# Seven block products on three PSUM banks: another order of products, evictions, masks and stores in an attention and FFN kernel

## The chip, the core and the metric

The kernel runs on one core of a Trainium2 chip. A core has TensorE (PE, with its weight loads listed as PEld), VectorE (DVE), ScalarE (ACT), GpSimd (POOL) and SyncE (SP), which here only issues transfers. Time is the device time of one execution in microseconds; lower is better. Beside it stands the span: from the first to the last instruction that the hardware profiler recorded in one execution.

## What is computed

Attention with two kinds of masks, then a feed-forward layer, on 8 batches of 576 tokens, 8 heads of 64:

```python
scores = scale * np.matmul(q, k.transpose(0, 1, 3, 2))
rel = pos[:, None] - pos[None, :]
mask_plain = (rel >= 0) & (rel < 32)                        # heads 0 to 3
mask_dil = (rel >= 0) & (rel < 128) & (rel % 4 == 0)        # heads 4 to 7
attn = softmax(np.where(masks, scores, -1e9))
x = matmul(attn, v) as (4608 tokens, 512)
h = np.maximum(x @ w_in, 0.0)                               # w_in 512 x 2048
out = h * h @ w_out                                         # w_out 2048 x 512
```

The output is 4608 x 512 in float32; the matmuls run in bfloat16.

## The kernel before

The 4608 tokens go through the feed-forward layer in nine tiles of 512. For a tile the first matmul (`mm1`, L963) makes 16 blocks of 128 hidden features, four matmuls each. ACT takes each block from PSUM with a Relu (L993) and DVE squares it (L996) into `h2T`. The second matmul then sums over the 16 blocks. Attention for a batch runs between: the list `steps` (L1317 to L1394) tells behind which group of matmuls which step of attention is issued, and `natural_step` (L697) issues it. A step is a visit of PE (`V`, function `quadrants`, matmuls at L377) with scores for some head pairs and products with V for others; or the exponential and mask of a pair (`E`, ACT at L740, DVE at L742); or a logarithm of the sums (`L`, L708 and L709); or a reciprocal by an exponential and the multiplication into `xT`, the feed-forward layer's input (`X`, ACT L723, DVE L726 and L730). The order within an engine is the order of issue: nothing is reordered later. Waits are set where a tile is read, written or its buffer reused, and PE, ACT and DVE each go through their queues in order.

Batch 7, the last, has its two visits inside the seventh tile: one between the two matmuls of the feed-forward layer, one in the middle of the second. They are the last attention work; tiles eight and nine are feed-forward alone.

In the last three tiles (`fast`, L954) the second matmul is done in blocks of two by two with seven products in place of eight. Hidden features (low, high) and the tokens' two interleaved halves make four blocks a11, a12, a21, a22 of `h2T`; `w_out` has four blocks b11 to b22. `add_up` (L1022) makes on DVE the sums s1 = a21 + a22, a21 := a11 - a21, s2 = s1 - a11 and s4 = a12 - s2, in three pieces, behind blocks 7, 11 and 15. `weigh` makes the four sums of weights ahead of time. The products, 16 matmuls of 256 columns each, are M1 = a11 b11, M2 = a12 b21, M3 = s4 b22, M4 = a22 w4, M5 = s1 w1, M6 = s2 w2, M7 = a21 w3, and the four quarters of the output are

```
c11 = M1 + M2                  c12 = M1 + M6 + M5 + M3
c21 = M1 + M6 + M4 + M7        c22 = M1 + M6 + M7 + M5
```

`PRODUCTS` (L1085) gives the order, M1, M2, M6, M4, M7, M5, M3, and the PSUM bank of each. Banks come from the pool `ps_f` with four buffers, which also serves `mm1` and the visits. M6 is added by PE onto M1's bank, so that this bank holds M1 + M6; each of the others has its own. `after` (L1048) takes products out: ACT copies M1 and later M1 + M6 into `snap`, DVE adds banks and `snap` into `whole`, a float32 image of the tile's output, whose four row blocks hold every fourth token. `keep` stores one row block of `whole` per transfer, from SP (L944). In the last tile M3 comes in three pieces with a bank each, and the stores are cut by quarters.

The names by which the profile shows the sums: s1 and s2 lie in `qb`, s4 in `kb`; w1 and w2 lie in `qb`, w3 and w4 in `kb`.

Of the kernel before, what the change touches and what calls it, by code (L numbers as in the profile page):

```python
# [63 lines left out]
def kernel(  # L64
# [631 lines left out]

    def natural_step(b: int, code: str):  # L697
        what, e = code[0], int(code[1])
        if what in "QKR":
            arrange(b, what, e, int(code[2]), *(int(x) for x in code[3:4]), *[nc.scalar.copy][: len(code) - 4])  # L700
        elif what == "V":
            scs, pvs = ([(int(x[0]), int(x[1])) for x in y.split(",") if x] for y in code[2:].split("/"))
# [17 lines left out]
        elif what == "X":  # L720
            o, _, rest = op.pop((b, e))
            rec = recs.pop((b, e))
            nc.scalar.activation(rec[:, :], rec[:, :], ACT.Exp, scale=-1.0)  # L723
            t0 = b * M % (RING // RES)
            tok = xT[:, e, :, t0 : t0 + M]
            nc.vector.tensor_tensor(out=tok[:, :, 16:M], in0=byr(o[:, :]), in1=byr(rec[:, 0:512]), op=ALU.mult)  # L726
            for g, rows in enumerate(sides) if rest[0][0] is not rest[0][1] else [(0, slice(0, P))]:
                if rest[0][0] is not rest[1][0]:
                    g = g ^ crossed(b, e)
                nc.vector.tensor_tensor(  # L730
                    out=tok[rows, :, 0:16], in0=byr(rest[0][g][rows, :]), in1=byr(rec[rows, 512:576]), op=ALU.mult
                )
        else:
            g = int(code[2])
            second = g ^ ((b, e) == (NATURAL, 1))
            if not second:
                pts[b, e] = p_pool.tile([P, 896], bf16, name="pt")
            n = 384 if e >= NE // 2 else (448, 384)[g]
            pt = pts[b, e][:, 448 * g : 448 * g + n]
            nc.scalar.activation(pt, sp[b, e][g][:, 0:n], ACT.Exp, scale=SCALE)  # L740
            mask = (mask_f if e >= NE // 2 else mask_p[:, 384:] if b == XB else mask_n)[:, 0:n]
            nc.vector.tensor_tensor(out=pt, in0=pt, in1=mask, op=ALU.mult)  # L742
# [15 lines left out]

    far_blocks = [[(0, 0, 0, 64)], [(0, 16, 64, 112), (1, 80, 80, M)]]
    recs, turned = {}, set()  # L760
    first = {}
    held = []
    sides = [slice(64 * hl, 64 * hl + 64) for hl in range(2)]
# [176 lines left out]
    def store(osb, parts, *cuts):  # L940

        for x, n, row in parts:
            for c0, c1 in zip(cuts, cuts[1:]):
                nc.sync.dma_start(out[row : row + RES * (n - 1) + 1 : RES, c0:c1], osb[x : x + n, c0:c1])  # L944

    def ffn_groups(tk0: int, nt: int):
# [16 lines left out]
        def mm1(u, ks):  # L963
# [51 lines left out]
        sums_at = {7: (0, 4), 11: (4, 6), 15: (6, 8)}  # L1015

        def quarter(f0, f1, high, j):
# [4 lines left out]
        def add_up(f0, f1):  # L1022
# [3 lines left out]
            for to, one, two_, op in (  # L1026
                (s1, a21, a22, ALU.add),
                (a21, a11, a21, ALU.subtract),
                (s2, s1, a11, ALU.subtract),
                (s4, a12, s2, ALU.subtract),  # L1030
            ):
                nc.vector.tensor_tensor(out=to, in0=one, in1=two_, op=op)  # L1032

        final = tk0 + nt == NTOK
# [3 lines left out]
        def plus(to, one, two_):  # L1038
            nc.vector.tensor_tensor(out=to, in0=one, in1=two_, op=ALU.add)  # L1039

        def keep(rows, *cuts):
            for m in rows:
                parts = [(0, half, tk0 + m + RES * half), (half, half, tk0 + m)] if over else [(0, P, tk0 + m)]
                store(whole[:, m, :], parts, *cuts)

        halves = (0, HD, DM)

        def after(name, pieces=None):  # L1048

            bank = {k: t[:, :, :] for k, t in cur.items()}  # L1050
            if name == "M1":
                nc.scalar.copy(snap[0][:, :, :], bank["X"])  # L1052
            elif name == "M2":
                plus(c11, bank["Z"], snap[0][:, :, :])
                if final:
                    keep((0, 2), 0, HD)
            elif name == "M6":
                nc.scalar.copy(snap[1][:, :, :], bank["X"])
            elif name == "M4":
                plus(c21, bank["W"], snap[1][:, :, :])  # L1060
            elif name == "M7":
                plus(c21, bank["V"], c21)
                if final:
                    keep((1, 3), 0, HD)
            elif name == "M5":
                plus(snap[0][:, :, :], bank["Y"], snap[1][:, :, :])
                plus(c22, bank["V"], snap[0][:, :, :])
                keep((1, 3), *((HD, DM) if final else (0, DM)))
# [7 lines left out]
        def summed(x):  # L1076
            return lambda f, i: h_sum[x][:, f, P * i : P * i + P]
# [4 lines left out]
        def w_of(x):  # L1082
            return lambda f: w_sum[x][:, f, :]

        PRODUCTS = {  # L1085
            "M1": ("X", raw(0, 0), w_raw(0, 0)),
            "M2": ("Z", raw(1, 0), w_raw(1, 0)),
            "M6": ("X", summed(1), w_of(1)),
            "M4": ("W", raw(1, 1), w_of(3)),
            "M7": ("V", raw(0, 1), w_of(2)),  # L1090
            "M5": ("Y", summed(0), w_of(0)),
            "M3": ("Q", summed(2), w_raw(1, 1)),
        }
        ITEMS = [(name, f, i, 0, HD) for name in PRODUCTS for f in range(NF // 2) for i in range(2)]
        if final:
            ITEMS[-NF:] = [
                ("M3", f, i, y0, y1) for i, y0, y1 in ((0, 0, HD), (1, 0, HD // 2), (1, HD // 2, HD)) for f in range(NF // 2)
            ]

        def g2_fast(n):  # L1100

            head_ = 4 * NF
            lo, hi = (8 * n, 8 * n + 8) if n < 8 else (head_ + 6 * n - 48, head_ + 6 * n - 42 if n < 15 else len(ITEMS))
            for name, f, i, y0, y1 in ITEMS[lo:hi]:
                bank, lhs, rhs = PRODUCTS[name]
                piece = final and name == "M3"
                begin = f == 0 and (piece or i == 0) and name != "M6"
                if begin:
                    cur[bank] = ps_f.tile([P, 2, HD], f32, name="pf")
                nc.tensor.matmul(  # L1110
                    cur[bank][:, i, y0:y1], lhs(f, i), rhs(f)[:, y0:y1], start=begin, stop=f == NF // 2 - 1, skip_group_check=True
                )
# [220 lines left out]
    for b in range(NATURAL, B):  # L1333
# [35 lines left out]
            norm(1, t + 25)  # L1369
        else:  # L1370
            visit(t + 15, [(b, 3), (b, 1)], [(b, 0), (b, 2)][: 1 + (b >= PAIRED)])
            steps.extend((t + 15, 3, b, f"E1{x}") for x in range(2))
            if b >= PAIRED:
                norm(2, t + 15)
            expo(3, t + 16, t + 16)
            norm(0, t + 17)
            visit(t + 23, [(b + 1, 2), (b + 1, 0)] if after else [], [(b, 1), (b, 3)])
            if after:
                steps.extend((t + 23, 3, b + 1, f"E0{x}") for x in range(2))
                steps.extend((t + 27 + 2 * x, 1, b + 1, f"E2{x}") for x in range(2))  # L1380
            norm(3, t + 23)
            norm(1, t + 24)
# [62 lines left out]
```

## Time and profile before

| | |
|---|---|
| median of three runs | 293.96 us (293.78 to 298.44) |
| the profiled execution | 294.17 us, span 292.4 us |
| PE busy | 282.7 us, 97% |
| DVE busy, ACT busy | 183.5 us, 184.4 us, 63% each |
| seventh tile, second matmul with both visits | about 219.8 to 235.8 us |
| eighth tile | 235.8 to 261.8 us |
| ninth tile to the end | 261.8 to 292.4 us |

A row of a timeline gives start, busy time, engine, line and operation, `out<-in` with shapes, a count, and in brackets how long the engine had been idle and what ended that. A row of the waits gives the sum, the count and the longest. A modelled end stands behind each matmul: matmuls overlap, so their starts tell the pace. DMA rows give the size of a transfer and the median time from issue to landing.

### The profile page before, as it was taken

The page shows a single profiled execution, that of the slowest core. Times are in us where ns is not written, and L with a number is a line of the kernel's source. Part 1 is how long each engine was busy: PE and PEld are TensorE (multiplying, and loading weights), DVE is VectorE, ACT ScalarE, POOL GpSimd, SP SyncE. Part 2 cuts the span into 40 slices and gives each one's busy share as a digit, 9 for nine tenths or more (in the row PEclk, how much of TensorE's full clock was granted, in tenths as well). Part 3 has the DMA queues.
Part 4 walks back from the last instruction along what each step waited for, and adds up shares of the span by engine and source line. Part 5 has one row for each costly group of instructions (what it writes and reads, how often), then busy time and mean ns, then how long its engine had stood idle before and what let it go on. Part 6 is the DMA issues. An engine that isn't in the chain of part 4 may idle for free.

```text
span 292.4 us, 8216 instructions
## 1 busy us (share of the span) xinstructions
PE 282.7 (97%) x3361; PEld 179.7 (61%) x3377; DVE 183.5 (63%) x494; ACT 184.4 (63%) x375; POOL 123.2 (42%) x208
## 2 busy tenths in 40 slices
PE   8899999999999999999999999999998999999994
PEld 7589746959555544555455455555556865885683
DVE  2676315646769665686749577975388457643943
ACT  6788627777747864988667666667566547307510
POOL 8685266755553892876774679100000000000000
PEclk9999999999999999999999999999999999999999
DMA  8999999999999999999999499202100040003013
GB/s 123 196 172 205 205 218 203 187 159 164 168 210 153 180 125 206 115 171 201 125 219 166 50 138 221 23 2 102 43 1 2 4 143 0 2 28 115 2 36 108
DMA packets 84180, 35.77 MB, mean 122 GB/s; under 512 B 53296, under 2 KB 79536, under 8 KB 84144
## 3 DMA queue, kind: packets, MB, share of 16 engines
q0 software_dynamic: 49056, 18.49, 58.4%
q1 hardware_dynamic: 34944, 16.67, 28.8%
q8 instruction: 26, 0.43, 0.6%
q10 hardware_dynamic: 144, 0.10, 0.1%
q14 instruction: 10, 0.08, 0.1%
HBM read 37.50 MB, written 9.44 MB: 161 GB/s over the span
## 4 chain that ended last, share of the span: by engine, by line
PE 88%; DVE 5%; DMA 2%; ACT 2%; issue 1%; POOL 1%; DVEq 0%; POOLq 0%
PE pf L980 39%; PE pf L1148 28%; PE pf L1110 11%; DMA kb<-in_k_dram 2%; PE po L377 2%; DVE h2T L996 2%; PE pa L377 1%; PE pf L377 1%; DVE qb L1032 1%; ACT h2T L993 1%; PE pd L377 1%; PE pa L804 1%; ACT pt L740 1%; DVE kb L1032 1%; PE pf L856 0%
## 5 line engine op out<-in xcount | busy, mean ns | idle before, releaser
L980 PE MATMUL pf<-xT,w_in 128*128 128x512 bf16 (+1 forms) x704 | 128.0, 341 | 0.0
L993 ACT ACTIVATE h2T<-pf 128x512 bf16<-128x512 f32 x143 | 84.0, 602 | 42.3 <-PE pf L980 42.1
L980 PEld LDWEIGHTS <-w_in 128*128 128x128 bf16 x704 | 78.2, 114 | 45.7 <-issue 0.3
L1148 PE MATMUL pf<-w_out_sb,h2T 128*128 128x512 bf16 x368 | 84.1, 379 | 1.4 <-issue 0.6
L996 DVE TENSOR_TENSOR h2T<-h2T 128x512 bf16<-128x512 bf16 (+1 forms) x123 | 55.9, 468 | 33.4 <-ACT h2T L993 31.7
L1148 PEld LDWEIGHTS <-h2T 128*128 128x128 bf16 x384 | 36.5, 98 | 42.3
L329 POOL DMA_DIRECT2D vbd<-in_v_dram x80 | 43.2, 550 | 23.9 <-DMA qb<-in_q_dram 10.8
L1154 ACT COPY osb<-pf 128x512 f32<-128x512 f32 x22 | 12.9, 585 | 20.8 <-PE pf L1148 20.8
L1110 PEld LDWEIGHTS <-h2T 128*128 128x128 bf16 x192 | 18.6, 98 | 2.6
L723 ACT ACTIVATE rec<-rec 128x576 f32<-128x576 f32 x24 | 16.4, 685 | 0.7
L740 ACT ACTIVATE pt<-pa 128x384 bf16<-128x384 f32 (+1 forms) x26 | 11.8, 499 | 6.7 <-DVE xT L730 6.0
L183 POOL DMA_DIRECT2D kb<-in_k_dram x19 | 13.1, 691 | 6.7 <-DMA w_in<-in_moe_w_in_dram 3.2
L205 POOL DMA_DIRECT2D vbd<-in_v_dram x16 | 11.0, 694 | 11.7 <-DMA kb<-in_k_dram 7.8
L183 POOL DMA_DIRECT2D qb<-in_q_dram x19 | 13.5, 712 | 4.7 <-DMA xx<-qb 2.6
L321 POOL DMA_DIRECT2D vbd<-in_v_dram x20 | 12.0, 610 | 7.0 <-DMA qb<-in_q_dram 2.6
L726 DVE TENSOR_TENSOR xT<-po,rec 128x512 bf16<-128x512 f32 x13 | 9.0, 691 | 6.9 <-ACT rec L723 6.6
L1039 DVE TENSOR_TENSOR whole<-pf,snap 128x512 f32<-128x512 f32 (+2 forms) x14 | 8.2, 612 | 7.9 <-PE pf L1110 7.8
L1110 PE MATMUL pf<-qb,qb 128*128 128x256 bf16 x96 | 11.5, 272 | 1.5 <-ACT snap L1052 1.5
L315 POOL DMA_DIRECT2D vd<-in_v_dram x20 | 12.1, 614 | 1.4 <-issue 0.5
L742 DVE TENSOR_TENSOR pt<-pt,mask_f 128x384 bf16<-128x384 bf16 x24 | 8.4, 355 | 6.4 <-ACT pt L740 6.3
L726 DVE TENSOR_TENSOR xT<-pf,rec 128x512 bf16<-128x512 f32 x11 | 7.6, 691 | 7.6 <-ACT rec L723 7.6
L742 DVE TENSOR_TENSOR pt<-pt,mask_n 128x384 bf16<-128x384 bf16 (+1 forms) x20 | 7.1, 373 | 7.5 <-ACT pt L740 7.4
(176 smaller groups left out, 382.2 us busy)
## 6 DMA issues: line engine op xcount, KB each, us to landing
out_dram<-osb SPq DMA_DIRECT2D x24, 128.0 KB, 5.0
out_dram<-osb SPq DMA_DIRECT2D x12, 256.0 KB, 4.7
qb<-in_q_dram POOLq DMA_DIRECT2D x7, 320.0 KB, 11.3
kb<-in_k_dram POOLq DMA_DIRECT2D x7, 320.0 KB
vd<-in_v_dram POOLq DMA_DIRECT2D x34, 64.0 KB, 6.2
w_out_sb<-in_moe_w_out_dram POOLq DMA_DIRECT2D x4, 512.0 KB
out_dram<-whole SPq DMA_DIRECT2D x8, 256.0 KB, 3.0
qb<-in_q_dram POOLq DMA_DIRECT2D x6, 256.0 KB, 6.3
```

Source lines behind the costliest of these rows:

```text
L183: nc.gpsimd.dma_start(t[p0 : p0 + n, part, h0:h1, :], src[b, h0:h1, t0 : t0 + RES * n, :].rearrange("h (p r) d -> p h (r d)", r=RES),)
L329: nc.gpsimd.dma_start(v_rows[b % 2][p0 + 16 * r : p0 + 16 * r + 16, e, :, :], v[b, 2 * e + hl, :, :].rearrange("(i m r) d -> r m i d", r=R ...
L377: nc.tensor.matmul(out, lhs, rhs, start=begin, stop=True, skip_group_check=True)
L723: nc.scalar.activation(rec[:, :], rec[:, :], ACT.Exp, scale=-1.0)
L726: nc.vector.tensor_tensor(out=tok[:, :, 16:M], in0=byr(o[:, :]), in1=byr(rec[:, 0:512]), op=ALU.mult)
L740: nc.scalar.activation(pt, sp[b, e][g][:, 0:n], ACT.Exp, scale=SCALE)
L742: nc.vector.tensor_tensor(out=pt, in0=pt, in1=mask, op=ALU.mult)
L980: nc.tensor.matmul(to, w_in_sb[piece][:, kt, c0 : c0 + 509 : 4], rhs, start=(kt == kts[0] and x == 0), stop=(kt == kts[-1] and x == per - ...
L993: nc.scalar.activation(hv, acc[u][:, :].rearrange("p (x n) -> p x n", x=per), ACT.Relu)
L996: nc.vector.tensor_tensor(out=hv, in0=hv, in1=hv, op=ALU.mult)
L1110: nc.tensor.matmul(cur[bank][:, i, y0:y1], lhs(f, i), rhs(f)[:, y0:y1], start=begin, stop=f == NF // 2 - 1, skip_group_check=True)
L1148: nc.tensor.matmul(cur[m][:, c0:c1], h2[:, f, P * m : P * m + P], w_out_sb[:, f, c0:c1], start=(f == 0), stop=(f == NF - 1),)
```

## The change

- The order of the products becomes M1, M5, M6, M3, M7, M2, M4, on three banks: X takes M1, then M6, M7 and M4 on top of it, Y takes M5 and M3 on top, Z takes M2. X and Y are allocated together, Y first, ahead of M1. PE adds four products onto a bank in use where it added one, and DVE does three sums per tile where it did six.
- Evictions: ACT copies X behind M1 into c11, Y behind M5 into c22, X behind M6 into c12 and X behind M4 into c21. DVE adds Y to c12 behind M3, X to c22 behind M7, Z to c11 behind M2. `snap` goes.
- In the last tile M4 comes in the three pieces, now all on bank X, each copied by ACT.
- `keep` stores two row blocks (0 and 2, or 1 and 3) in one transfer.
- In the seventh tile: pair 1 of batch 7 does its second half's exponential first; its masks (`m`) are issued later than its exponentials (`e`); pair 3's exponentials and pair 0's normalisation come one and two groups later; the last `add_up` does s1 and s2 first and a21 and s4 (`Z0`) behind the masks.

```diff
-    snap = [const.tile([P, 2, HD], f32, name=f"snap{x}") for x in range(2)]
...
-            second = g ^ ((b, e) == (NATURAL, 1))
-            if not second:
-                pts[b, e] = p_pool.tile([P, 896], bf16, name="pt")
+            second = g ^ ((b, e) in ((NATURAL, 1), (B - 1, 1)))
             n = 384 if e >= NE // 2 else (448, 384)[g]
+            if "m" not in code:
+                if not second:
+                    pts[b, e] = p_pool.tile([P, 896], bf16, name="pt")
+                pt = pts[b, e][:, 448 * g : 448 * g + n]
+                nc.scalar.activation(pt, sp[b, e][g][:, 0:n], ACT.Exp, scale=SCALE)
+            if "e" in code:
+                return
...
-                add_up(*sums_at[u])
+                put_off = visited and u == NF - 1
+                add_up(*sums_at[u], (0, 2) if put_off else (0, 1, 2, 3))
+                if put_off:
+                    late.append(lambda: add_up(*sums_at[u], (1, 3)))
...
+        def keep(m, c0, c1, n=2):
+
+            to = out[tk0 : tk0 + NT, :].rearrange("(p m) c -> p m c", m=RES)
+            nc.sync.dma_start(to[:, m : m + 2 * n - 1 : 2, c0:c1], whole[:, m : m + 2 * n - 1 : 2, c0:c1])
+
+        def after(name):
...
             if name == "M1":
-                nc.scalar.copy(snap[0][:, :, :], bank["X"])
+                nc.scalar.copy(c11, bank["X"])
+            elif name == "M5":
+                nc.scalar.copy(c22, bank["Y"])
+            elif name == "M6":
+                nc.scalar.copy(c12, bank["X"])
+            elif name == "M3":
+                plus(c12, bank["Y"], c12)
+                if final:
+                    keep(0, HD, DM)
+            elif name == "M7":
+                plus(c22, bank["X"], c22)
+                if final:
+                    keep(1, HD, DM)
             elif name == "M2":
-                plus(c11, bank["Z"], snap[0][:, :, :])
...
+                plus(c11, bank["Z"], c11)
+                keep(0, 0, HD if final else DM)
             elif not final:
-                plus(c12, bank["Q"], snap[0][:, :, :])
-                keep((0, 2), 0, DM)
+                nc.scalar.copy(c21, bank["X"])
+                keep(1, 0, DM)
...
             "M1": ("X", raw(0, 0), w_raw(0, 0)),
+            "M5": ("Y", summed(0), w_of(0)),
+            "M6": ("X", summed(1), w_of(1)),
+            "M3": ("Y", summed(2), w_raw(1, 1)),
+            "M7": ("X", raw(0, 1), w_of(2)),
             "M2": ("Z", raw(1, 0), w_raw(1, 0)),
+            "M4": ("X", raw(1, 1), w_of(3)),
...
+            if n == 0:
+                for bank in "YX":
+                    cur[bank] = ps_f.tile([P, 2, HD], f32, name="pf")
...
-                    cur[bank][:, i, y0:y1], lhs(f, i), rhs(f)[:, y0:y1], start=begin, stop=f == NF // 2 - 1, skip_group_check=True
+                    cur[bank][:, i, y0:y1], lhs(f, i), rhs(f)[:, y0:y1],
+                    start=name in ("M1", "M5", "M2") and f == i == 0, stop=f == NF // 2 - 1, skip_group_check=True,
...
-                if piece:
-                    plus(c12[:, i, y0:y1], cur[bank][:, i, y0:y1], snap[0][:, i, y0:y1])
-                    keep((2 * i,), HD + y0, HD + y1)
+                if final and name == "M4":
+                    nc.scalar.copy(c21[:, i, y0:y1], cur[bank][:, i, y0:y1])
+                    if y1 == HD:
+                        keep(2 * i + 1, 0, HD, 1)
...
-            steps.extend((t + 15, 3, b, f"E1{x}") for x in range(2))
+            if after:
+                steps.extend((t + 15, 3, b, f"E1{x}") for x in range(2))
+            else:
+                steps.extend((t + 15, 3, b, f"E1{x}e") for x in (1, 0))
+                steps.extend((t + 16, 1, b, f"E1{x}m") for x in (1, 0))
+                steps.append((t + 16, 2, b, "Z0"))
...
-            expo(3, t + 16, t + 16)
-            norm(0, t + 17)
+            expo(3, *[t + 17 - after] * 2)
+            norm(0, t + 19 - 2 * after)
```

More of the change, by code (lines that the diff above doesn't have):

```diff
@@ L698, in natural_step @@
         what, e = code[0], int(code[1])
-        if what in "QKR":
+        if what == "Z":
+            late.pop()()
+        elif what in "QKR":
             arrange(b, what, e, int(code[2]), *(int(x) for x in code[3:4]), *[nc.scalar.copy][: len(code) - 4])
@@ L760 @@
     recs, turned = {}, set()
+    late = []
     first = {}
@@ L1012, in mm1 @@
             if fast and u in sums_at:
-                add_up(*sums_at[u])
+                put_off = visited and u == NF - 1
+                add_up(*sums_at[u], (0, 2) if put_off else (0, 1, 2, 3))
+                if put_off:
+                    late.append(lambda: add_up(*sums_at[u], (1, 3)))
         sums_at = {7: (0, 4), 11: (4, 6), 15: (6, 8)}
+        visited = tk0 == FAST * NT
         def quarter(f0, f1, high, j):
@@ L1020, in quarter, with add_up @@
             return blocks_of[:, j, f0:f1, :, :]
-        def add_up(f0, f1):
+        def add_up(f0, f1, which):
             s1, s2, s4 = (x[:, f0:f1, :].rearrange("p f (i t) -> p f i t", t=P) for x in h_sum)
             a11, a12, a21, a22 = (quarter(f0, f1, high, j) for j in range(2) for high in range(2))
-            for to, one, two_, op in (
+            todo = (
                 (s1, a21, a22, ALU.add),
@@ L1030, in add_up @@
                 (s4, a12, s2, ALU.subtract),
-            ):
+            )
+            for to, one, two_, op in (todo[x] for x in which):
                 nc.vector.tensor_tensor(out=to, in0=one, in1=two_, op=op)
@@ L1096, in ffn_groups @@
             ITEMS[-NF:] = [
-                ("M3", f, i, y0, y1) for i, y0, y1 in ((0, 0, HD), (1, 0, HD // 2), (1, HD // 2, HD)) for f in range(NF // 2)
+                ("M4", f, i, y0, y1) for i, y0, y1 in ((0, 0, HD), (1, 0, HD // 2), (1, HD // 2, HD)) for f in range(NF // 2)
             ]
@@ L1103, in g2_fast @@
             lo, hi = (8 * n, 8 * n + 8) if n < 8 else (head_ + 6 * n - 48, head_ + 6 * n - 42 if n < 15 else len(ITEMS))
+            if n == 0:
+                for bank in "YX":
+                    cur[bank] = ps_f.tile([P, 2, HD], f32, name="pf")
             for name, f, i, y0, y1 in ITEMS[lo:hi]:
                 bank, lhs, rhs = PRODUCTS[name]
-                piece = final and name == "M3"
-                begin = f == 0 and (piece or i == 0) and name != "M6"
-                if begin:
+                if bank not in cur:
                     cur[bank] = ps_f.tile([P, 2, HD], f32, name="pf")
                 nc.tensor.matmul(
-                    cur[bank][:, i, y0:y1], lhs(f, i), rhs(f)[:, y0:y1], start=begin, stop=f == NF // 2 - 1, skip_group_check=True
+                    cur[bank][:, i, y0:y1], lhs(f, i), rhs(f)[:, y0:y1],
+                    start=name in ("M1", "M5", "M2") and f == i == 0, stop=f == NF // 2 - 1, skip_group_check=True,
                 )
@@ L1381 @@
             norm(3, t + 23)
-            norm(1, t + 24)
+            norm(1, t + 25 - after)
         at = t - (14 if b < PAIRED else 19 if b == PAIRED else 25)
```

26 lines of the change are left out of this document (removed).

## The prediction

> **What bounds the kernel now.** I read the page first, then the list of waits, the chain that ended last, and the timelines of PE, ACT and DVE in the three tiles that the change touches.
>
> ```profile
> span 292.4 us, 8216 instructions
> PE 282.7 (97%) x3361; PEld 179.7 (61%) x3377; DVE 183.5 (63%) x494; ACT 184.4 (63%) x375; POOL 123.2 (42%) x208
> PEclk9999999999999999999999999999999999999999
> ```
>
> PE is busy for 97% of the span at full granted clock, so time goes only with PE work, PE waits, or what lies behind PE's last matmul. The matmuls are the same in number and shape before and after, so PE work is fixed. In the built program nothing differs up to the seventh tile's last squares, at about 220 us. The chain in the 73 us behind that point reads (columns: start, us, what):
>
> ```profile
> 235.96 13.81 PE pf L980 x64
> 249.77 12.23 PE pf L1110 x112
> 262.00 13.81 PE pf L980 x64
> 275.81 10.49 PE pf L1110 x96
> ...
> 286.33 0.70 DVE snap L1039
> 287.03 0.02 issue
> 287.05 1.22 DVE whole L1039 x3
> 288.27 0.20 DVEq L1440
> ```
>
> From 235.96 on PE runs without a break. The seven products of the eighth tile are 112 matmuls in 12.23 us, 0.1092 us each, 1.75 us for a product of 16. So the eighth tile can give nothing. What is left are the seventh tile's wait and the tail. The waits of PE have one row there:
>
> ```profile
> PE pf L1110 <- ACT snap L1052: 1.5, 1, 1.5
> ```
>
> **The seventh tile.** PE:
>
> ```profile
> 221.03 3.67 PE L1110 MATMUL pf<-w_out_sb,h2T 128*128 128x256 bf16 x32
> 226.16 1.91 PE L1110 MATMUL pf<-qb,qb 128*128 128x256 bf16 x16 [1.46 <-ACT snap L1052]
> 227.90 1.91 PE L1110 MATMUL pf<-kb,h2T 128*128 128x256 bf16 x16
> 229.74 0.23 PE L377 MATMUL po<-pt,vbd 64*64 64x96 bf16 x2
> 230.54 1.92 PE L1110 MATMUL pf<-kb,h2T 128*128 128x256 bf16 x16
> ```
>
> M1 and M2 begin at 221.03, and 32 matmuls later, at 221.03 + 32 x 0.1092 = 224.52, M6 could begin on M1's bank. It begins at 226.16: 1.64 us lost (the row's 1.46 counts from the modelled end). ACT shows why M1's copy (L1052) is late:
>
> ```profile
> 220.43 0.92 ACT L740 ACTIVATE pt<-pf 128x448 bf16<-128x448 f32 x2
> 222.00 0.69 ACT L723 ACTIVATE rec<-rec 128x576 f32<-128x576 f32 x1
> 224.75 0.87 ACT L740 ACTIVATE pt<-pa 128x384 bf16<-128x384 f32 x2 [2.07 <-DVE xT L730]
> 225.51 0.59 ACT L1052 COPY snap<-pf 128x512 f32<-128x512 f32 x1
> 226.76 0.68 ACT L723 ACTIVATE rec<-rec 128x576 f32<-128x576 f32 x1
> 230.67 0.60 ACT L708 ACTIVATE rec<-pf 128x512 f32<-128x512 f32 x1 [1.99 <-PE pd L377]
> ```
>
> The copy stands in ACT's queue behind two exponentials that wait 2.07 us for DVE's L730, and DVE reaches L730 late because additions and masks stand ahead of it:
>
> ```profile
> 222.16 0.42 DVE L1032 TENSOR_TENSOR qb<-qb,h2T 128x512 bf16<-128x512 bf16 x1
> 222.96 0.65 DVE L742 TENSOR_TENSOR pt<-pt,mask_n 128x448 bf16<-128x448 bf16 x2
> 223.90 0.69 DVE L726 TENSOR_TENSOR xT<-pf,rec 128x512 bf16<-128x512 f32 x1
> 224.50 0.22 DVE L730 TENSOR_TENSOR xT<-pa,rec 128x64 bf16<-128x64 f32 x1
> 227.47 0.69 DVE L726 TENSOR_TENSOR xT<-po,rec 128x512 bf16<-128x512 f32 x1 [1.20 <-ACT rec L723]
> 232.13 0.69 DVE L726 TENSOR_TENSOR xT<-pf,rec 128x512 bf16<-128x512 f32 x1 [1.52 <-ACT rec L723]
> ```
>
> **The change, part by part.** *Order and exponentials.* In the built program ACT does E11, E10, logarithms and exponential of pair 2, then M1's copy, and only then pair 3's exponentials. ACT is free at 222.00 + 0.69 = 222.69; M1's issue ends at 221.03 + 1.75 = 222.78. In the eighth tile a copy begins 0.20 us behind that point (rows below: 249.61 + 1.75 = 251.36, copy at 251.56), and PE resumes 0.06 us behind a copy's end (226.16 against 225.51 + 0.59). So the copy runs 222.98 to 223.57 and M6 may start at 223.63. M5 stands between and ends at 224.52: hidden, with 0.90 us to spare. The wait of 1.64 us goes. E11 (384 columns, not 448) now frees M1's bank; by the mean of 0.46 us in the row at 220.43 that is some 0.04 us sooner. Gain 1.68.
>
> *Masks and additions put back.* DVE does s1 and s2, then the normalisation of pair 2 at 222.72 (once ACT has its reciprocal) to 223.54, then masks (0.65), their sums, a21 and s4. That is 222.72 + 0.69 + 0.22 + 0.65 + 0.34 + 2 x 0.42, about 225.3 with overlaps. s4 is needed in M3 from 226.27, a21 in M7: hidden by M6. Pair 3's masks end near 226.3 and the second visit needs them at 228: hidden by M3.
>
> *What is late next.* M5's copy is a new instruction in ACT's queue and waits for M5: 224.52 + 0.20 = 224.72. Behind it stand pair 0's logarithms and reciprocal, and behind these DVE's normalisation, which frees the bank that the second visit writes first. In the row at 225.51 the step from a copy's start to that normalisation is 227.47 - 225.51 = 1.96 us; now it begins at 226.68 and is through, L730 with it, at 227.5. The visit is due at 221.0 + 4 x 1.75 + 0.1 = 228.1, so 0.5 us is left: the tightest place. M2's bank is freed by M3's sum (228.3 to 229.0; due 230.6). M7's sum stands behind pair 3's normalisation: the visit's start plus 2.39 (232.13 - 229.74), so 230.4 + 0.9, then 0.69, about 231.9; M4 is due at 232.3. The eighth tile then starts 1.68 us earlier.
>
> *Eighth and ninth tile.* M5 now follows M1 and needs s1; M6 needs s2:
>
> ```profile
> 249.61 3.66 PE L1110 MATMUL pf<-w_out_sb,h2T 128*128 128x256 bf16 x32
> 251.23 0.42 DVE L1032 TENSOR_TENSOR qb<-h2T 128x512 bf16<-128x512 bf16 x1
> 251.56 0.59 ACT L1052 COPY snap<-pf 128x512 f32<-128x512 f32 x1 [1.15 <-PE pf L1110]
> 252.03 0.42 DVE L1032 TENSOR_TENSOR qb<-qb,h2T 128x512 bf16<-128x512 bf16 x1
> ```
>
> s1's last piece is there at 251.65, and M5 reads it with its 13th matmul, 249.61 + 28 x 0.1092 = 252.67; s2 is there at 252.45 and M6 starts at 253.10. Both hidden, by 1.0 and 0.65 us. Each of the four handovers of a bank in use costs 0.20 + 0.59 (a sum 0.69) + 0.06, that is 0.85 to 0.95 us, under a product of 1.75. Cost 0. Per tile ACT has two copies more and DVE three sums fewer; both sit idle between products. Stores of the seventh and eighth tile go in two transfers in place of four, the first 1.75 us earlier; the next writer of `whole` is a tile later: 0.
>
> *The tail.* Here the change adds two PE waits. M4's three pieces lie in one bank, and the built program lets each piece wait for the copy of the one before. The rows are PE's and SP's timelines, a group of ACT and two groups of transfers (count, size, us to landing).
>
> ```profile
> 286.13 1.93 PE L1110 MATMUL pf<-w_out_sb,kb 128*128 128x256 bf16 x24
> 287.77 2.29 SPq L944 DMA_DIRECT2D out_dram<-whole  x5
> 289.66 0.40 SPq L944 DMA_DIRECT2D out_dram<-whole  x1
> L709 ACT ACTIVATE rec<-pa 128x64 f32<-128x64 f32 x4 | 1.0, 239 | 0.0
> out_dram<-whole SPq DMA_DIRECT2D x7, 128.0 KB, 2.0
> out_dram<-whole SPq DMA_DIRECT2D x8, 256.0 KB, 3.0
> ```
>
> Before, PE was through at 288.06, but five stores queue on SP and the last is issued at 289.66. After, in the same clock: piece 1 ends at 286.13 + 8 x 0.1092 = 287.00. Eight half-width matmuls take (1.93 - 0.87 - 0.17) / 2 = 0.45. A copy of 256 or 128 columns has no row; between 0.24 (64 columns) and 0.59 (512) a straight line gives 0.39 and 0.29. So 287.00 + 0.20 + 0.39 + 0.06 + 0.45 + 0.20 + 0.29 + 0.06 + 0.45 + 0.20 + 0.29 = 289.59, and SP, now with no queue, issues the last store at about 289.62: 0.04 earlier. With all copies at 0.24 it is 0.25 less, with all at 0.59 it is 0.80 more; the short copies are nearest to the 64-column row. The last store has 128 KB in place of 64. From 256 to 128 KB the landing falls by 1.0 us, so 64 KB would be at most 0.5 quicker; these rows had others in flight, and I take 0.1. Tail: +0.06, between -0.3 and +1.3.
>
> With a bank for each piece the last copy would end near 288.4 and the store go 1.2 us sooner; that is what sharing costs here. The Trainium skill, "Perfetto Trace Analysis", section "Matmuls", says so as a rule: independent groups should rotate through banks, so that one is evicted under the next. Here no run so far has such pieces on one bank; by the page's rule the sum would be 1.2 us lower with rotated banks, as just worked out from the rows, and the wait at 226.16 agrees with it in kind.
>
> Sum: -1.64 - 0.04 + 0.06 = -1.62. The profiled execution took 294.17 us (span 292.4), 0.21 over the median of 293.96; so 292.55 against the first and 292.3 against the median.
>
> **The rivals.** *The wait moves.* The second visit's first weights wait for pair 0's normalisation, 0.5 us ahead by my sum. What ACT or DVE lose beyond that comes off the gain; 2.1 us late would eat it all: 293.9. For it: three dependent engines in a row. Against: every duration is from rows of this tile.
>
> *Slower: banks in use.* If evictions could not run under the product between, each of four handovers in three tiles would cost PE 0.85: 12 x 0.85 = 10.2, so 302.5. It decides once an eviction starts 0.9 us late. Against: M6 on M1's bank already works so in the eighth and ninth tile, and the list of waits has no row for it. [...]
>
> *The tail is dearer.* Copies near 0.59 and a slow last store: 292.3 + 0.8 = 293.1. For it: PE now stops twice, and no row shows these copies.
>
> **How the numbers follow.** Forecast 0.74, moved wait 0.10, dearer tail 0.12, slower 0.04. The range goes from 293.96 - 1.68 - 0.3 = 292.0, less 0.2 for the spread of the two lower runs (293.78, 293.96) and 0.2 for overlaps read off the rows, so 291.6, to the moved wait, 293.9. About 2%, 5.9 us, is what a measurement of this kernel can tell from no change. Only rival two crosses it, on the slow side; on the fast side PE's fixed work leaves nothing of that size: faster 0.01, same 0.95, slower 0.04.
>
> **What would show it.** In the changed profile: no wait of PE for a copy before 235 us; M5 directly behind M1; the eighth tile's first matmul at about 234.1 in place of 235.79; the second visit without a wait; 112 matmuls in 12.2 us in the eighth tile; at the end two gaps of PE of 0.5 to 0.7 us, each ended by ACT, and SP's last store near 288.0. Wrong would be: a wait of PE before the second visit, a gap at any handover in the eighth tile, or an end that keeps its distance from the last product less well than computed.

## The result

The changed kernel takes 292.33 us (median of 20 runs) where the kernel before, timed beside it, takes 294.02 (20 runs). The ratio is 0.9952, with a 95% interval of 0.9932 to 0.9972: 1.7 us faster, less than the 2% that the chances went by. The forecast of 292.3 is 0.03 us off, closer than the interval, some 0.6 us to either side, can vouch for.

One line that the diff under "The change" does not show turns out to matter. In the last batch, pair 1's normalisation also comes one group later:

```diff
-            norm(1, t + 24)
+            norm(1, t + 25 - after)
```

### The profile after

The page of the changed kernel, and its waits of PE (sum, count, longest), of which only this row lies behind 220 us:

```profile
span 290.5 us, 8217 instructions
PE 284.7 (98%) x3377; PEld 180.1 (62%) x3377; DVE 177.4 (61%) x483; ACT 187.9 (65%) x383; POOL 122.9 (42%) x208
```

```profile
PE pf L1119 <- ACT whole L1126: 0.9, 2, 0.5
```

The span is 1.82 us shorter (290.54 and 292.36 before it is rounded). The old row, 1.5 us for `snap`, is gone; the new one is the pair of waits in the tail. PE's timeline of the seventh tile (start, busy time, what) has M1, then M5 and M6, M3, the second visit, M7, M2, M4 and the eighth tile:

```profile
220.76 1.92 PE L1119 MATMUL pf<-w_out_sb,h2T 128*128 128x256 bf16 x16
222.52 3.66 PE L1119 MATMUL pf<-qb,qb 128*128 128x256 bf16 x32
226.01 1.91 PE L1119 MATMUL pf<-w_out_sb,kb 128*128 128x256 bf16 x16
227.85 0.23 PE L376 MATMUL po<-pt,vbd 64*64 64x96 bf16 x2
...
228.65 1.92 PE L1119 MATMUL pf<-kb,h2T 128*128 128x256 bf16 x16
...
232.16 1.91 PE L1119 MATMUL pf<-kb,h2T 128*128 128x256 bf16 x16
233.90 2.32 PE L986 MATMUL pf<-xT,w_in 128*128 128x512 bf16 x10
```

From M1 to the eighth tile: 233.90 - 220.76 = 13.14 us; before, 235.79 - 221.03 = 14.76. M1 itself starts 0.27 earlier, in code that the change leaves alone (spread between executions), and the tail takes 0.07 back: from the last product's first matmul to the end of the span it is 290.54 - 284.24 = 6.30 us, before 292.36 - 286.13 = 6.23. So 1.62 + 0.27 - 0.07 = 1.82. For this comparison of places I take off the 0.27 wherever the prediction gave an absolute time.

ACT's timeline of the same stretch, and then DVE's:

```profile
222.72 0.59 ACT L1061 COPY whole<-pf 128x512 f32<-128x512 f32 x1 [0.31 <-PE pf L1119]
223.29 0.87 ACT L742 ACTIVATE pt<-pa 128x384 bf16<-128x384 f32 x2
224.46 0.59 ACT L1063 COPY whole<-pf 128x512 f32<-128x512 f32 x1 [0.30 <-PE pf L1119]
224.94 0.60 ACT L709 ACTIVATE rec<-pd 128x512 f32<-128x512 f32 x1
```

```profile
223.05 0.21 DVE L731 TENSOR_TENSOR xT<-pa,rec 128x64 bf16<-128x64 f32 x1
223.18 0.65 DVE L747 TENSOR_TENSOR pt<-pt,mask_n 128x384 bf16<-128x384 bf16 x2
...
226.41 0.69 DVE L727 TENSOR_TENSOR xT<-po,rec 128x512 bf16<-128x512 f32 x1 [0.74 <-ACT rec L724]
227.02 0.21 DVE L731 TENSOR_TENSOR xT<-pa,rec 128x64 bf16<-128x64 f32 x1
...
230.98 0.68 DVE L1050 TENSOR_TENSOR whole<-pf,whole 128x512 f32<-128x512 f32 x1
231.58 0.68 DVE L727 TENSOR_TENSOR xT<-po,rec 128x512 bf16<-128x512 f32 x1
```

M1's copy now stands ahead of pair 3's exponentials and waits only for PE. Pair 0's normalisation ends at 227.02 + 0.21 = 227.23, and the visit that needs it begins at 227.85: 0.6 us are left. M7's sum (230.98) stands ahead of pair 1's normalisation (231.58), which is the work of the line shown above.

The chain of the changed kernel behind that point, and the end of its timeline:

```profile
234.07 13.81 PE pf L986 x64
247.88 12.23 PE pf L1119 x112
260.11 13.81 PE pf L986 x64
273.92 11.37 PE pf L1119 x104
```

```profile
284.24 1.04 PE L1119 MATMUL pf<-kb,h2T 128*128 128x256 bf16 x8
...
285.36 0.37 ACT L1126 COPY whole<-pf 128x256 f32<-128x256 f32 x1 [5.57 <-PE pf L1119]
285.78 0.61 PE L1119 MATMUL pf<-kb,h2T 128*128 128x128 bf16 x8 [0.50 <-ACT whole L1126]
...
286.74 0.61 PE L1119 MATMUL pf<-kb,h2T 128*128 128x128 bf16 x8 [0.35 <-ACT whole L1126]
...
287.38 0.27 ACT L1126 COPY whole<-pf 128x128 f32<-128x128 f32 x1 [0.69 <-PE pf L1119]
```

The eighth tile's 112 matmuls take the same 12.23 us on three banks as on their own banks before. In the tail PE stops twice, and SP issues the last store at 287.67, 3.43 us behind 284.24 (before 289.66 - 286.13 = 3.53).

### The profile page after: what moved, and what is told of

Read it like the earlier page. It is cut to its first block, busy times and chain, and to the rows that moved or that the text cites. A ratio compares the mean times of both kernels' runs of the same rounds, so it can differ in the third digit from the quotient of the medians.

```text
span 290.5 us, 8217 instructions
## 1 busy us (share of the span) xinstructions
PE 284.7 (98%) x3377; PEld 180.1 (62%) x3377; DVE 177.4 (61%) x483; ACT 187.9 (65%) x383; POOL 122.9 (42%) x208
## 4 chain that ended last, share of the span: by engine, by line
PE 91%; DMA 5%; issue 1%; ACT 1%; DVE 1%; POOL 0%; ACTq 0%; POOLq 0%
PE pf L986 41%; PE pf L1159 27%; PE pf L1119 13%; DMA kb<-in_k_dram 3%; PE po L780 2%; DMA vbd<-in_v_dram 2%; PE po L376 2%; PE pf L376 1%; PE pa L376 1%; PE pa L810 1%; PE pd L376 1%; DVE vbd L254 0%; PE pf L862 0%; ACT whole L1126 0%; PE pf L840 0%
## 5 line engine op out<-in xcount | busy, mean ns | idle before, releaser
L1159 PE MATMUL pf<-w_out_sb,h2T 128*128 128x512 bf16 x384 | 85.6, 379 | 0.1
L1050 DVE TENSOR_TENSOR whole<-pf,whole 128x512 f32<-128x512 f32 x9 | 6.2, 690 | 12.7 <-PE pf L1119 12.7
L1119 PE MATMUL pf<-kb,h2T 128*128 128x256 bf16 (+1 forms) x104 | 11.8, 264 | 0.9 <-ACT whole L1126 0.9
```

What stands on the lines that cost most here:

```text
L1119: nc.tensor.matmul(cur[bank][:, i, y0:y1], lhs(f, i), rhs(f)[:, y0:y1], start=name in ("M1", "M5", "M2") and f == i == 0, stop=f == NF // ...
L1159: nc.tensor.matmul(cur[m][:, c0:c1], h2[:, f, P * m : P * m + P], w_out_sb[:, f, c0:c1], start=(f == 0), stop=(f == NF - 1),)
```

## The experiments

My theory was the prediction's: all of the gain is M6's wait in the seventh tile, removed by the order of steps there; banks in use cost nothing where a product stands between; what sharing one bank costs is in the tail. The rivals: the new products bring part of the gain; the stores do; there is no margin before the second visit, or a large one.

### Each half of the change alone

**The steps alone.** The kernel before, with its products, banks, `snap` and stores, and of the change only `natural_step`, the split `add_up` and the list of steps:

```diff
-            steps.extend((t + 15, 3, b, f"E1{x}") for x in range(2))
+            if after:
+                steps.extend((t + 15, 3, b, f"E1{x}") for x in range(2))
+            else:
+                steps.extend((t + 15, 3, b, f"E1{x}e") for x in (1, 0))
+                steps.extend((t + 16, 1, b, f"E1{x}m") for x in (1, 0))
+                steps.append((t + 16, 2, b, "Z0"))
...
-            norm(1, t + 24)
+            norm(1, t + 25 - after)
```

> The kernel before with only the seventh tile's steps changed: exponentials of pair 1 ahead of its masks, pair 3's exponentials behind M1's copy, a21 and s4 put behind the masks. Products, banks, evictions and stores are those of before. Theory (the step order alone takes away the wait): M1's copy stands ahead of pair 3's exponentials, runs at about 223.0, and M6, due at 224.52, does not wait: 1.64 us less than before, about 292.4, the same as the whole change. Rival (the order of products and the reuse of banks makes the gain): no change from before, 294.0, with PE's wait of about 1.5 us for the copy still in the list.

Measured: 292.53 us, ratio 0.9951 (0.9930 to 0.9973); before 293.74, timed beside it. PE's timeline has M1 with M2, then M6 without a wait, and the eighth tile:

```profile
220.38 3.67 PE L1122 MATMUL pf<-w_out_sb,h2T 128*128 128x256 bf16 x32
223.88 1.91 PE L1122 MATMUL pf<-qb,qb 128*128 128x256 bf16 x16
...
233.52 2.75 PE L987 MATMUL pf<-xT,w_in 128*128 128x512 bf16 x12
```

233.52 - 220.38 = 13.14, the very figure of the whole change. The steps, with the line for pair 1's normalisation among them, are the whole gain.

**The changed kernel again**, timed beside the same runs of the kernel before:

> The changed kernel itself, for comparison on the same chip: 0.993 to 0.997 of before, and the last store 3.4 us behind M4's first matmul.

Measured: 292.42, ratio 0.9949 (0.9926 to 0.9971). From M1 to the eighth tile it is 234.35 - 221.21 = 13.14 us once more, and the tail is again 6.30.

**The products alone.** The changed kernel with the steps put back:

```diff
-                put_off = visited and u == NF - 1
+                put_off = False
...
-            expo(3, *[t + 17 - after] * 2)
-            norm(0, t + 19 - 2 * after)
+            expo(3, t + 16, t + 16)
+            norm(0, t + 17)
...
-            norm(1, t + 25 - after)
+            norm(1, t + 24)
```

> The changed kernel with the seventh tile's steps as before (X allocated ahead of Y, as pair 1's first half is again freed first). Products, three banks, evictions and stores are the changed ones. Theory: pair 3's exponentials stand again ahead of M1's copy, which starts near 225.5; M6, now third as before, waits for it about 1.5 us by the list, and M3 may wait 0.15 us more for M5's copy behind pair 0's reciprocal: 293.9 to 294.3, no gain. Rival (products and banks make the gain): 292.3.

Measured: 295.14, ratio 1.0040 (1.0018 to 1.0061): slower than before, which I had not expected. Its waits of PE, and two rows of its timeline, DVE's and PE's:

```profile
PE pf L1119 <- ACT whole L1061: 1.5, 1, 1.5
```

```profile
233.52 1.28 DVE L1050 TENSOR_TENSOR whole<-pf,whole 128x512 f32<-128x512 f32 x2
...
234.25 1.91 PE L1119 MATMUL pf<-kb,h2T 128*128 128x256 bf16 x16 [0.71 <-DVE whole L1050]
```

The old wait is there, and M4 has one of its own: M4 is added onto M7's bank, and M7's sum on DVE comes behind pair 1's normalisation, at 233.52. M2 began at 231.63, so M4 was due at 231.63 + 1.75 = 233.38 and lost 0.87. From M1 (220.31) to the eighth tile (235.99) it takes 15.68, 0.92 more than before; what the medians differ by beyond that lies within the interval. So the new order of products creates a reader that the old one did not have, and one line of the steps exists to serve it.

**The products and that line.** The same kernel with pair 1's normalisation one group later:

```diff
-            norm(1, t + 24)
+            norm(1, t + 25 - after)
```

> The new products, banks and stores with the old order of steps in the seventh tile, as in the run with the products alone, but pair 1's normalisation one group later, as the change has it. Theory: in the run with the products alone two waits stood against each other, M6's for M1's copy (the old one, 1.64 us) and M4's for M7's sum, which stood on DVE behind pair 1's normalisation (0.87 us of the stretch). The second goes now: the stretch from M1's start to the eighth tile takes 14.8 us (before 14.76, products alone 15.68), no wait of PE for DVE's sum, and the median is 294.3 by the run with the products alone less 0.87, or 294.0 by the kernel before plus 0.05; I take 294.1, ratio 1.000 to 1.002. Rival: the products cost something else there (a ratio that stays at 1.004, about 295.1).

Measured: 294.02 beside 293.89, ratio 1.0000 (0.9980 to 1.0019). The wait for DVE's sum is gone from the waits of PE, and behind 220 us the old one stands alone with the tail's:

```profile
PE pf L1119 <- ACT whole L1061: 1.5, 1, 1.5
...
PE pf L1119 <- ACT whole L1126: 0.9, 2, 0.5
```

M1 at 220.84, eighth tile at 235.67: 14.83. The miss is explained: products, banks and stores together are worth nothing here, to 0.2% either way.

### Which step removes the wait

**Pair 3's exponentials put back** ahead of M1's copy, the rest as changed:

```diff
-            expo(3, *[t + 17 - after] * 2)
+            expo(3, t + 16, t + 16)
```

> The changed kernel with pair 3's exponentials back ahead of M1's copy; the first half's exponential order, the masks put back and the additions put back stay. Theory: the old wait of 1.64 us had two parts, the place of M1's copy behind these exponentials and their own wait for a normalisation that stood behind masks and additions on DVE. With the masks put back that normalisation ends at 223.3 in the changed kernel's time; two exponentials of 0.87 together then let M1's copy end at 224.75 and M6 starts 224.8 instead of 224.25: a wait of about 0.55 us, median 292.95. Rivals: the place of the copy is the whole of it (the full 1.64 comes back, 294.0); it is nothing once the masks are put back (292.4).

Measured: 292.80, ratio 0.9965 (0.9953 to 0.9977). ACT's rows and then PE's:

```profile
223.59 0.87 ACT L742 ACTIVATE pt<-pa 128x384 bf16<-128x384 f32 x2 [0.89 <-DVE xT L731]
224.35 0.59 ACT L1061 COPY whole<-pf 128x512 f32<-128x512 f32 x1
```

```profile
221.06 1.92 PE L1119 MATMUL pf<-w_out_sb,h2T 128*128 128x256 bf16 x16
...
224.99 1.91 PE L1119 MATMUL pf<-qb,qb 128*128 128x256 bf16 x16 [0.27 <-ACT whole L1061]
```

The exponentials still wait for L731, but 0.89 us where it was 2.07, since masks and additions no longer stand ahead of it on DVE. M6 starts 3.93 behind M1 instead of 3.50, and the eighth tile 13.57 behind it instead of 13.14. With the other steps in place, then, the exponentials' place is worth 0.43 of the 1.62 us; the other steps take away 1.2 without it, and ACT's wait that fell from 2.07 to 0.89 says that it is the masks and additions put back. The theory held, with 0.43 for 0.55. These are shares in this one order of undoing, not prices of the parts: ahead of the exponentials M1's copy waits for PE alone (222.72 in the changed kernel), so moving the exponentials without the masks might have removed most of the wait as well. Neither the exponentials alone nor the masks alone were run.

### The margin before the second visit

**M5's copy four times** in the seventh tile:

```diff
-                nc.scalar.copy(c22, bank["Y"])
+                for _ in range(4 if visited else 1):
+                    nc.scalar.copy(c22, bank["Y"])
```

> The changed kernel with M5's copy of the seventh tile done four times in place of once: three copies more on ACT, 0.48 us each in a row, ahead of pair 0's logarithms. It measures what is left before the second visit has to wait. Theory: pair 0's normalisation ends about 0.5 us ahead of the visit, so of 1.45 us about 0.9 come through to PE: 0.9 us more than the changed kernel, 293.2, with a wait of PE before the second visit. Rival (the old wait has moved to the second visit already): all 1.45 us come through, 293.8. Third (something else covers it): nothing comes through, 292.3.

Measured: 293.88, ratio 1.0006 (0.9985 to 1.0028), 1.46 over the changed kernel timed beside it (292.42). The design was not clean. The copies also hold bank Y, and M3 waits for it:

```profile
227.16 1.91 PE L1120 MATMUL pf<-w_out_sb,kb 128*128 128x256 bf16 x16 [0.78 <-ACT whole L1064]
```

I had overlooked that second reader, so this run alone could not separate the two. The next one does.

**Other work in the same place on ACT**: three copies of 512 columns behind M5's copy that read no bank.

```diff
                 nc.scalar.copy(c22, bank["Y"])
+                for _ in range(3 if visited else 0):
+                    nc.scalar.copy(c21, c11)
```

> The changed kernel with three more copies of 512 columns on ACT (from c11 to c21, which M4's copy overwrites later) behind M5's copy in the seventh tile, so that neither bank is held longer. Theory: pair 0's normalisation, which the second visit waits for, has 0.6 us left. An SBUF copy of 512 columns has no row; between 0.45 and 0.6 us each the delay is 1.35 to 1.8, so M3's start keeps its place, the visit starts 0.75 to 1.2 us late and the median is 293.2 to 293.6. In any case the loss in the stretch from M1 to the eighth tile is the delay of pair 0's logarithm (seen on ACT) less 0.6. Rivals: no margin left (loss equal to the delay, 293.8 to 294.2); a margin of 1.3 or more, so that nothing is lost (292.4).

Measured: 293.65, ratio 1.0000 (0.9980 to 1.0019) to the kernel before, 293.89 here; some 1.2 to 1.3 us over the changed kernel. ACT and then PE:

```profile
225.28 1.92 ACT L1065 COPY whole<-whole 128x512 f32<-128x512 f32 x3
227.10 0.59 ACT L709 ACTIVATE rec<-pd 128x512 f32<-128x512 f32 x1
```

```profile
229.40 0.42 PE L376 MATMUL po<-pt,vbd 64*64 64x96 bf16 x2 [1.14 <-DVE xT L731]
230.41 1.92 PE L1121 MATMUL pf<-kb,h2T 128*128 128x256 bf16 x16
```

M1 began at 221.09 here and M3 kept its place. Pair 0's logarithm starts 227.10 - 221.09 = 6.01 behind M1, where it was 224.94 - 220.76 = 4.18: a delay of 1.83. The visit starts 8.31 behind M1, where it was 7.09: 1.22 late. So 0.61 us were left, as read off the changed kernel's trace, and both rivals (no margin, a large one) fall. The run with four copies gives the same, 1.86 less 1.25. The eighth tile came 1.43 late, 0.2 more than expected: from the visit's start to M7 it takes 1.01 us in both runs, against 0.80 in the changed kernel. All of the 0.2 lies between the visit's first matmul and those behind it, which start 0.23 us later in this run (229.40 and 229.63) and 0.01 later in the changed kernel (227.85 and 227.86). Why, stays open. Counted at the eighth tile, 0.4 of the 1.83 was covered.

### Banks in use

**M6 directly behind M1, M3 directly behind M5**, in all three tiles:

```diff
             "M1": ("X", raw(0, 0), w_raw(0, 0)),
-            "M5": ("Y", summed(0), w_of(0)),
             "M6": ("X", summed(1), w_of(1)),
+            "M5": ("Y", summed(0), w_of(0)),
             "M3": ("Y", summed(2), w_raw(1, 1)),
```

with X allocated ahead of Y.

> The changed kernel with the products in the order M1, M6, M5, M3, M7, M2, M4 on the same three banks: M6 follows M1 directly on X, and M3 follows M5 directly on Y, so nothing lies between a product and the next one on its bank. Theory: two handovers in each of three tiles now show in full, 0.20 + 0.59 + 0.06 = 0.85 us each, 5.1 us in all: 297.4, and PE's list of waits has six rows' worth of copies of 0.6 us or so. Rival (PE adds onto a bank while ACT still reads it, or the copy is otherwise covered): 292.3.

Measured: 298.22 (four runs, 296.93 to 301.33), ratio 1.0126 (1.0090 to 1.0162); 297.4 was expected. The chain in the eighth tile:

```profile
253.55 1.76 PE pf L1119 x16
255.33 0.59 ACT whole L1061
255.93 0.04 issue
255.97 3.67 PE pf L1119 x32
259.66 0.59 ACT whole L1063
260.25 0.04 issue
260.30 7.15 PE pf L1119 x64
```

267.44 - 253.55 = 13.89 us for the seven products, against 12.23: 0.83 for each exposed handover, six of them 5.0. In the profiled execution, the slowest of the four and 9.0 longer in span than the changed kernel's, the seventh tile's M1 already starts 3.9 us late, in code that is the same; the rest is about the 5.0. The two fastest runs lie 4.6 and 4.8 over the changed kernel's 292.33. A bank in use is free with one product of 1.75 us between and costs 0.83 without.

### The tail

**Two banks for the last product**, one for each half, so that nothing in M4 waits:

```diff
-                for bank in "YX":
+                for bank in "YXW" if final else "YX":
...
+                bank = "W" if final and bank == "X" and i else bank
...
-            ITEMS[-NF:] = [
-                ("M4", f, i, y0, y1) for i, y0, y1 in ((0, 0, HD), (1, 0, HD // 2), (1, HD // 2, HD)) for f in range(NF // 2)
-            ]
+            ITEMS[-NF:] = [("M4", f, i, 0, HD) for i in range(2) for f in range(NF // 2)]
```

> The changed kernel; in the last tile X is two banks, one for each half of the tokens, and M4 comes in two pieces of 256 columns, one on each, with no wait of PE between. Theory (the pieces' shared bank costs the tail): the last copy of 256 columns (0.37 us) ends 0.2 + 0.37 us behind PE's last matmul, and the last store is issued 2.35 us behind M4's start in place of 3.43: 1.1 us less than the changed kernel, 291.2. Rival (the end is set by the landing of the stores before it): the last store is issued earlier but the end stays, 292.3.

Measured: 291.27, ratio 0.9905 (0.9888 to 0.9922) to the kernel before: faster than both kernels (the changed kernel, in other runs, had 0.9952, 0.9932 to 0.9972). No wait of PE in the tail; its timeline ends with:

```profile
284.62 1.91 PE L1128 MATMUL pf<-kb,h2T 128*128 128x256 bf16 x16
...
286.56 0.37 ACT L1135 COPY whole<-pf 128x256 f32<-128x256 f32 x1 [0.45 <-PE pf L1128]
```

The last copy ends 2.31 behind M4's first matmul, against 3.41 in the changed kernel, and the tail is 289.99 - 284.62 = 5.37 against 6.30. So 1.1 us sooner on ACT became 0.9 at the end of the span. M4 also comes in two pieces here and not in three; three pieces on three banks were not run.

**One piece on one bank**, copied as a whole:

```diff
-            elif not final:
+            else:
                 nc.scalar.copy(c21, bank["X"])
-                keep(1, 0, DM)
+                keep(1, 0, HD if final else DM)
```

> The changed kernel; in the last tile M4 is one piece on X with one copy of 512 columns and one store of 256 KB. Theory: the last store is issued 1.75 + 0.20 + 0.59 + 0.03 = 2.57 us behind M4's start in place of 3.43, and lands some 0.4 us more slowly (2.5 against 2.1 us): 0.45 us less than the changed kernel, 291.9. Rival (cutting the last product in pieces is worth its waits): slower than the changed kernel by 0.3 us or more, 292.6.

Measured: 292.24, ratio 0.9938 (0.9921 to 0.9955). The copy ends at 286.34 + 0.59 = 286.93, 2.58 behind M4's start (284.35), yet the tail is 290.44 - 284.35 = 6.09, only 0.21 less, where 0.45 was expected: the last store is 256 KB in place of 128 and lands later.

### The stores

**A transfer for each row block**, otherwise as changed, run twice:

```diff
-            nc.sync.dma_start(to[:, m : m + 2 * n - 1 : 2, c0:c1], whole[:, m : m + 2 * n - 1 : 2, c0:c1])
+            for x in range(m, m + 2 * n - 1, 2):
+                nc.sync.dma_start(to[:, x, c0:c1], whole[:, x, c0:c1])
```

> The changed kernel with one row block per transfer, as before: four stores in place of two in the seventh and eighth tile, eight in place of five in the last. Theory: no store but the last lies on the path, and SP is free when the last is due: 292.3, the last store still 3.4 us behind M4's start. Rival (fewer issues on SP is what keeps the tail even): up to three issues of 0.45 us queue ahead of the last, 0.3 to 1.0 us more.

> The changed kernel with a transfer for each row block, a second time. It first measured 292.91 (5 undisturbed runs) with a last store issued as early as in the changed kernel. Theory: the number of transfers costs nothing, 292.4; rival: the 0.5 us are there again, 292.9, and the last store lands about 0.8 us later.

Measured: 292.91, ratio 0.9975 (0.9945 to 1.0005), then 293.19, ratio 0.9985 (0.9969 to 1.0001). The theory of no cost falls: the medians are 0.6 and 0.9 us over the changed kernel's 292.33, though the intervals overlap and the runs were not timed beside each other. In the trace it is clearer. The last store is issued as early as in the changed kernel (3.44 behind M4's start), but the tail is 7.09 and 6.81, where the changed kernel and five other runs with its three pieces of M4 and its stores have 6.30. Transfers between 286.5 and 292 us, in 40 slices of 0.1375 us, of the changed kernel and then of the first of these runs, each with the row for the instruction queue in the same stretch (packets, MB, share of the engines' time):

```profile
GB/s 350 343 350 357 306 350 350 127 0 0 0 0 0 0 82 335 365 164 8 0 0 0 0 0 0 0 0 0 0 0 0 0 0 60 0 0 0 0 0 0
...
q14 instruction: 1, 0.01, 0.5%
```

```profile
GB/s 335 350 209 8 0 0 0 0 0 0 22 253 395 253 30 0 0 7 22 22 7 0 0 0 0 0 0 0 0 0 0 0 0 0 0 0 0 0 0 0
...
q14 instruction: 1, 0.01, 0.9%
```

The last store is the second hump. In the changed kernel nothing follows it within the span (the 60 lies behind 290.5). With separate stores a straggler, a late rest of the store, goes on at 22 GB/s, a sixteenth of the 350 at full rate and so probably on one of the sixteen DMA engines. It ends 0.8 us behind the hump; the second run shows one that ends 0.7 us behind. That accounts for the longer tail: the span ends 1.4 to 1.5 us behind the last packet in all three.

The records of single DMA packets tell what it waits for. The row q14 is one packet of 8 KB that brings instructions. In the changed kernel it starts 6.82 us behind M4's first matmul, 2.0 behind the end of the last store. With separate stores it starts 4.47 behind it in both runs, inside the last store, and takes 0.77 and 0.63 us; the store's last eight packets of 1 KB follow one another from its end on. The records do not name the engine, but this is what one engine would show that serves both queues in turn. In the two runs of the margin, with three more copies on ACT, the packet starts at 2.13, ahead of the last store, and the tail is 6.30. The kernel with the steps alone, whose stores go row block by row block too, has no such packet in its tail, which takes 6.23. So the traces put the loss down to the instruction packet that falls into the last store and not to the number of transfers as such. What sets its place stays open.

## Why the prediction was right

- *M6's wait goes, 1.64 and 0.04.* Measured 1.62 from M1 to the eighth tile, and the steps alone give the same. The places that the gain hangs on came out within 0.02 us once the 0.27 is taken off: M1's copy 222.71 (222.72), M5's copy 224.45 (224.46), the normalisation's end 227.23 (227.23), the second visit 227.83 (227.85). The durations were rows of the same engines in the same tile, and their order was read off the built program. The 0.04 for the half of 384 columns first is not there: M1 starts 1.20 us behind the first visit's first matmul in both kernels (221.03 - 219.83 and 220.76 - 219.56). The trace's sum is 1.62 - 0.07 = 1.55 where 1.62 was forecast and the medians give 1.69; that the forecast fits the median to 0.03 us is luck.
- *What is late next.* 0.5 us was forecast before the second visit; 0.6 was there, and 0.61 by taking it away. M7's sum was forecast to end at 231.9 less 0.27, and ends at 231.66. This step came out right for a reason that it did not name, and so far by luck: it put M7's sum behind pair 3's normalisation alone, which holds only since pair 1's was moved back. That line was not priced, and without it M4 loses 0.87.
- *Handovers of a bank in use cost 0.* Right: 12.23 us in the eighth tile. Forecast at 0.85 to 0.95 each if exposed, they measured 0.83 in the run that exposed six.
- *The rule on banks.* The page "Perfetto Trace Analysis" of the Trainium skill, section "Matmuls", asks for a rotation of banks between independent groups, so that one is evicted under the next. The runs agree: 0.83 us each where the next product on the bank follows directly, 0.9 in the tail. The new order keeps the rule on two banks already: X, Y, X, Y rotates, each product is evicted under one on another bank, and the seven products take 12.23 us both ways.
- *The tail, +0.06 between -0.3 and +1.3.* Measured +0.07. The copies took 0.37 and 0.27 where 0.39 and 0.29 were interpolated; the last store went at 287.67, forecast 288.0 less 0.27. What a bank for each piece would bring was put at 1.2 us; two banks brought 1.1 on ACT and 0.9 in the span.
- *The stores cost 0.* The sum came out, but as a statement on the form of the stores it was wrong: with twice as many stores of one row block the tail is 0.5 and 0.8 us longer, in step with a transfer of instructions that then falls into the last store. No term of the prediction had it.

## What to carry to other kernels

Where PE waits for a bank, follow the copy that frees it back through the queue that it stands in: here the 1.62 us were bought by moving exponentials, masks and additions that had nothing to do with the product, while a new order of products and banks was worth nothing. A bank may be reused without cost when one product (1.75 us here) longer than the handover (0.83 us) stands between and the eviction is not late in its own queue, but each reuse adds a reader whose place in the eviction engine's queue has to be checked. Behind the last product nothing covers an eviction, so spare banks belong there.

## What the runs showed of the hardware

- Four copies of one bank to one place on ACT start 0.62 us apart (224.68, 225.30, 225.91, 226.53 in the run with M5's copy four times), each behind the end of the one before, and three from SBUF to SBUF 0.65 apart. The logarithm behind the four, on other tiles, starts 0.48 after the last of them, before that copy's end; so does the one behind M5's copy in the changed kernel (224.94 - 224.46). Whether the place read or the place written makes the difference is not shown.
- A visit whose first matmul had to wait took 1.01 us to the next product, one that had not 0.80, with the same instructions; the 0.2 lies behind the first matmul.
- Where a transfer of 8 KB of instructions (0.77 and 0.63 us) fell into the last store, eight packets of 1 KB of that store came 0.8 and 0.7 us behind the rest, and the tail was 7.09 and 6.81 us in place of 6.30.
